# A fused two-convolution, joint-network forward and backward kernel: row-layout fe by a transposing transfer in every second chunk, x loaded without its halo block, a longer warm-up, and two weights on another queue

## The chip, the cores and the metric

The kernel runs on one core of one Trainium2 chip. The metric is the device time of one execution in microseconds. Times below are device times, or spans of the profiled execution where they are called that.

## What is computed

The reference computes a small speech network and the gradients of all its inputs with respect to a given `grad_out`. Cut to what matters:

```python
# x (2,16000,256)  w1,w2 (3,256,256)  g (2,8,256)  w_f,w_g,w_o (256,256), all bf16
h  = gelu(sum_i xp[:, i:i+T] @ w1[i])[:, ::2]     # 3-tap convolution, every 2nd row kept
f  = gelu(sum_i hp[:, i:i+T1] @ w2[i])[:, ::2]    # the same again: 4000 rows per batch
fe = f @ w_f;  ge = g @ w_g
j  = tanh(fe[:, :, None, :] + ge[:, None, :, :])  # (2,4000,8,256)
out = j @ w_o
# out_0 = out, then the gradients of x, w1, w2, g, w_f, w_g, w_o
```

The two batches of 4000 rows at quarter rate make 8000 rows in all. Every one of them has 8 values of `u` (the 8 rows of `g`), so the joint part (tanh, the product with `w_o` and its gradients) is eight times as large as the rows suggest.

## The kernel before

**Chunks.** The 8000 quarter-rate rows are cut into 17 chunks: 15 of 4 blocks of 128 rows (512 rows), one of 2 blocks of 128, and a last one of 64. Chunk 7 holds the border of the two batches. Tiles come in two layouts. In the column layout the 256 channels lie on the partitions (two halves of 128) and rows lie along the free axis; matmuls of the forward pass and of the input gradients read it. In the row layout 128 rows lie on the partitions; the weight gradients read it, since they contract over rows.

**Stages.** `stage_a(g)` does chunk g's forward part: `conv1` for the odd rows and then for the even rows of h, `conv2`, and the product with `w_f`, which gives FE in column layout (L607). `stage_j(g)` does the joint part in four pairs of two u's: JT = tanh(FE + GE) in column layout on ScalarE (L676), JR, the same values in row layout, by an addition of FER and GEB on VectorE (L700) and a tanh on ScalarE (L705), the products with `w_o` transposed (GOT) and with `w_o` (OUT), and the gradient of `w_o` (GWO, from JR and GO). `stage_de(g)` does the backward part: GN, GH, the gradients of the weights and of x. The loop at L1282 calls `stage_j(k)`, `stage_a(k+1)` and `stage_de(k-1)` together, so that three chunks are in work at any time.

**Who sets the order.** Nothing is issued as it is written. `op` records an operation with its engine or engines, a cost, a due time (`F.now` or `at`), what it reads and writes and which buffers it opens. `Flow.issue` (L108) then plays a list schedule: of all operations that could start it takes the earliest, with the due time as a tie-breaker (and as the choice among SyncE's transfers that could start within `NEAR` ns of the first), and emits each on its engine's in-order queue. Numbers such as `0.424 * dt`, `q * 0.813`, `NEAR`, `CROWD` and `KAPPA` belong to this planner and are in ns or in shares of a chunk; they move instructions but add none. Nearly all DMAs are issued by SyncE (SP), whose queue is in order too: an instruction that waits holds all that stand behind it.

**What the change touches.**

- `load_xc` (L405) brings x of a chunk in column layout into XC with one transposing transfer of 17 blocks of rows. Block 0 holds the row before each group of 16, which is the same data as block 16 shifted by one. `rows_xc` (L379) does chunk 0 in another way: four plain transfers into XL, TensorE transposes (L399), copies out of PSUM, and a GpSimd copy for block 0.
- `fe_rows` (L610) makes FER, the row layout of FE, by 8 TensorE transposes per chunk of four blocks (L622, 4 for the chunk of two) into one PSUM tile and one copy to SBUF by ScalarE or VectorE (`evac`, L624). Chunks 1 to 15 have it; chunk 0 makes JR from JT by transposes (L694), and the last chunk has its own code (`stage_j_last`).
- `tile_rows` (L535) makes a row layout by a transposing transfer from SBUF to SBUF on SyncE. HR, GNR and GHR are made so.
- `halo` (L477) copies a shifted block and a saved last column with GpSimd instructions of the form 128x254 and 128x2 (all on L357).
- At the start, `warm_up` (L1210) issues 14 matmuls on zeros, whose result nobody reads, and `unread` (L370, with `FILL = (1, 3)`) puts one more such matmul behind the transposes of the first XL tile and three behind those of the second. W1, WF and WG are loaded from ScalarE's queue, W2 and WO from SyncE's.

All matmuls stand on the helper's line L322, DMAs on L346 (transposing) and L348 (plain), copies out of PSUM on L331 and L333 (ScalarE) and L336 and L338 (VectorE).

Of the kernel before, what the change touches and what calls it, by code (L numbers as in the profile page):

```python
# [36 lines left out]
class Flow:  # L37
# [6 lines left out]
    NEAR = 9.118  # L44
    COLD = 6000.0
    CROWD = 9000.0
    KAPPA = 0.0287
# [170 lines left out]
def kernel(  # L218
# [28 lines left out]
    KT = 2  # L247
# [30 lines left out]
    for name, n in (("xc", 1), ("ht", 1), ("g1e", 2), ("g1o", 2), ("g2", 2), ("fe", 2),  # L278
                    ("fer", 2), ("gsq", 3), ("gs", 2), ("jt", 3), ("got", 3), ("go", 4), ("out", 3), ("jr", 3),
                    ("hr", 2), ("jsq", 2), ("ngz", 2), ("gh", 1), ("gn", 1), ("gnr", 1), ("ghr", 1), ("xr", 1), ("gx", 2),  # L280
                    ("hho", 2), ("hg1", 2), ("hgf", 2), ("hge", 2)):
# [89 lines left out]
    FILL = (1, 3)  # L371
# [10 lines left out]
    def rows_xc(c, XC, at):  # L382
# [3 lines left out]
        for h in range(nr // 4):  # L386
            XL, r0 = XLS[h // 2], 4 * (h % 2)
            src = xf[0:nr * P, :].rearrange("(p r) d -> p r d", r=nr)[:, 4 * h:4 * h + 4, :]
            xl_ops.append(dma("SP", lambda XL=XL, r0=r0: XL[:, r0:r0 + 4, :], lambda src=src: src, r=[], w=[(XL, h % 2)], bytes_=P * 2048,
                new=[XL] if h % 2 == 0 else [], load=True, at=at - 2.0, land=-400.0))  # L390
# [17 lines left out]
    def load_xc(g_, at, apart=0.0):  # L408
        c = chunks[g_]
        XC = st[g_]["XC"] = buf("xr" if c.first else "xc", [P, 17, KT, P], BF16, "XC")  # L410
        if c.first:
            return rows_xc(c, XC, at)
        cuts = ((0, 4 * c.nb + 1),)
        for n_, (b0, b1) in enumerate(cuts):
# [3 lines left out]
                land=1500.0 if g_ == 1 else 4500.0)  # L418
        if c.mid:
            pool_zero(lambda: XC[:, 0, :, c.pb:c.pb + 1], [], [(XC, ("m", 0))], at=at)  # L420
# [56 lines left out]
    def conv_gelu(g_, jobs, rd, h_buf, pre, ho, gname, gcls, gshape, gsave, news):  # L477
# [36 lines left out]
        late = F.now + CW * ({0: 1.024, 2: 0.207, 1: 1.404}.get(g_, 0.36))  # L514
# [34 lines left out]
    def stage_a(g_, t0, dt):  # L549
# [23 lines left out]
        F.now = t0 + 0.0781 * dt  # L573
# [3 lines left out]
        F.now = t0 + 0.00759 * dt  # L577
# [32 lines left out]
        F.now = t0 + 0.84 * dt  # L610
        tile_rows(g_, "HR", "hr", HT, 3 * nb + 1, shape=[P, 3 * NB + 1, D], land=4500.0)

    def fe_rows(g_):
        c, S = chunks[g_], st[g_]
        nb, n_, FE = c.nb, c.np, S["FE"]
        FER = S["FER"] = buf("fer", [P, NB, D], BF16, "FER")
        ps = psum(BF16)

        def trs(e, ps=ps):
            for a in range(nb):  # L620
                for kt in range(KT):
                    nc.tensor.transpose(out=ps[:n_, (a * KT + kt) * P:(a * KT + kt + 1) * P],  # L622
                                        in_=FE[:, kt, a * n_:(a + 1) * n_], identity=ident[:])
# [36 lines left out]
    def stage_j(g_, t0, dt):  # L660
# [4 lines left out]
        def cut(ap, lo, hi):  # L665
            return ap.rearrange("p (a n) -> p a n", a=nb)[:, :, lo:hi] if c.mid else ap

        def pair(up):
# [4 lines left out]
            for j in range(2):  # L673
                for mt in range(KT):
                    for k_, (lo, hi, b) in enumerate(parts_of(c)):
                        op("ACT", c_act((hi - lo) * nb, ptr=True), lambda e, j=j, mt=mt, lo=lo, hi=hi, b=b: nc.scalar.activation(  # L676
                            out=cut(JT[:, j, mt, :W], lo, hi), in_=cut(S["FE"][:, mt, :W], lo, hi), func=ACT.Tanh,
                            bias=GE[:, b, mt, 2 * up + j:2 * up + j + 1], scale=1.0),
                           r=[(S["FE"], mt), (GE, b)], w=[(JT, (j, mt, k_))],
                           new=[JT] if j == 0 and mt == 0 and k_ == 0 else [], at=tu - q * (0.813 - (2 * j + mt) / 4))  # L680
            npart = len(parts_of(c))
            for h in range(max(nb // 2, 1)):
                na = min(nb, 2)
                JR = buf("jr", [P, 2, 2, D], BF16, "JR")
                th = tu + q * (h / 2 - 0.656)
# [30 lines left out]
                gwo_ops.append(op("PE", c_pe([V] * (4 * na)), gwo, r=[JR, GO], w=[], at=tu + q * (h / 2 + 0.468) + DEFER.get((g_, up), 0.0)))  # L716
            OUT = buf("out", [P, NB, 2, V], BF16, "OUT_SB")
            for step in range(4):
# [12 lines left out]
                if d2 == 0:  # L731
                    JSQ = buf("jsq", [P, KT, CW], BF16, "JSQ")

                    def jsq(e, j=j, JSQ=JSQ):
# [5 lines left out]
                       r=[(JT, (j, mt, k_)) for mt in range(KT) for k_ in range(npart)], w=[JSQ], new=[JSQ], at=F.now - q * 0.269)  # L740
# [58 lines left out]
    def stage_j_last(t0):  # L799
# [7 lines left out]
        for u in range(U):  # L807
            for mt in range(KT):
                op("ACT", c_act(n_, ptr=True), lambda e, u=u, mt=mt: nc.scalar.activation(
                    out=JT[:, 0, mt, u * n_:(u + 1) * n_], in_=S["FE"][:, mt, :n_], func=ACT.Tanh,  # L810
# [124 lines left out]
    def stage_de(g_, t0, dt):  # L935
# [15 lines left out]
        F.now = t0 + dt * 0.07  # L951
# [68 lines left out]
        load_xr(g_, t0 - 300.0 if c.last else t0 + dt * 0.382, [got_op[0, UP - 1]] if c.first else ())  # L1020
# [170 lines left out]
    X1 = -258.2  # L1191
    W0 = chunks[0].W
    H0 = 263.4
    CONVS = 4
    LEAD = 0.403
    LATE = (100.0, 100.0, 100.0)
    DEFER = {(LAST - 1, 3): 100.0, (LAST - 1, 2): 130.0}
    EARLY = 0.0
    GEBX = 0.93
# [8 lines left out]
    WARM = 14  # L1208
# [14 lines left out]
    wload("ACT", WF, 0, lambda: WF[:], lambda: w_f.rearrange("(kt p) n -> p kt n", p=P), BIG, 4000.0)  # L1223
    wact([wload("ACT", WG, 0, lambda: WG[:], lambda: w_g.rearrange("(kt p) n -> p kt n", p=P), BIG, 4000.0)])
    for b in range(B):
# [3 lines left out]
        r=[], w=[(W2, i) for i in range(KK)], bytes_=393216, load=True, at=BIG - 1.0, land=1000.0, behind=[xl_ops[-1]])  # L1229
    dma("SP", lambda: WO[:], lambda: w_o.rearrange("(kt p) n -> p kt n", p=P), r=[], w=[(WO, 0)], bytes_=131072, load=True,  # L1230
# [115 lines left out]
```

## Time and profile before

| what | value |
|---|---|
| median of 3 runs | 768.4 us (768.23 to 768.64) |
| the profiled execution's own time | 769.64 us |
| its span, first to last instruction | 767.9 us |
| granted TensorE clock over the span | 1.00 |
| TensorE matmuls (PE) busy | 761.4 us, 99% |
| VectorE (DVE) busy | 714.5 us, 93% |
| ScalarE (ACT) busy | 700.2 us, 91% |
| GpSimd (POOL) busy | 76.7 us, 10% |
| HBM read, written | 53.52 MB, 50.35 MB |

The profiled execution is 1.24 us longer than the median of the unprofiled runs. PE is matmul work, PEld the weight loads that overlap it; "idle before" is the time an engine stood still ahead of an instruction, with what ended it. The share of the DMA engines in this profile can go over 1, since packets of one engine overlap. SPq, ACTq and POOLq are the issuing sequencers of those engines.

### The profile page before, as it was taken

How to read it: one execution, taken by the hardware profiler on the slowest of the kernel's cores; microseconds unless marked ns; L12 is line 12 of the kernel's file. 1: busy time of each engine (PE TensorE's matmuls, PEld its weight loads, DVE VectorE, ACT ScalarE, POOL GpSimd, SP SyncE). 2: the span in 40 equal slices, each digit the busy share in tenths (PEclk: the TensorE clock that was granted, in tenths of full speed). 3: DMA queues.
4: the chain of work that ended last, by engine and by line, in shares of the span. 5: the costliest groups of instructions: out<-in, count | busy, mean ns of one | idle time of the engine just before them, and what ended most of it. 6: DMA issues, size and time to landing. Idle time of an engine off the chain costs nothing.

```text
span 767.9 us, 15189 instructions
## 1 busy us (share of the span) xinstructions
PE 761.4 (99%) x5564; PEld 529.0 (69%) x5564; DVE 714.5 (93%) x1480; ACT 700.2 (91%) x1137; POOL 76.7 (10%) x222
## 2 busy tenths in 40 slices
PE   9999999999999999999999999999999999999998
PEld 6576676767767576675766767567576776777785
DVE  4999999899998999989999999998899989899996
ACT  5999999999898998999999999998989989998843
POOL 1101100020110100002000020110101101010100
PEclk9999999999999999999999999999999999999999
DMA  9999999999999999999999999999999999997966
GB/s 240 219 245 238 260 221 234 232 250 267 261 245 250 263 255 224 258 251 238 239 253 249 265 245 223 280 240 245 224 247 245 234 277 211 246 267 200 215 165 156
DMA packets 392431, 183.80 MB, mean 239 GB/s; under 512 B 315961, under 2 KB 385252, under 8 KB 390437
## 3 DMA queue, kind: packets, MB, share of 16 engines
q1 hardware_dynamic: 390210, 181.83, 103.7%
q10 hardware_dynamic: 2050, 0.98, 0.4%
q8 instruction: 43, 0.70, 0.4%
q14 instruction: 32, 0.26, 0.1%
q0 software_dynamic: 96, 0.02, 0.0%
HBM read 53.52 MB, written 50.35 MB: 135 GB/s over the span
## 4 chain that ended last, share of the span: by engine, by line
PE 95%; ACT 2%; DVE 2%; DMA 1%; issue 1%; POOL 0%; SPq 0%; DVEq 0%; ACTq 0%
PE ps L322 79%; PE GWO L322 14%; PE psb L622 1%; DMA XL<-in_x_dram 1%; PE psb L694 0%; ACT GX_SB L333 0%; DVE NGZ L745 0%; PE psb L399 0%; ACT JSQ L736 0%; ACT OUT_SB L331 0%; ACT JT L676 0%; DVE g_s L509 0%; PE psb L1242 0%; DVE GN L760 0%; DVE ZS L760 0%
## 5 line engine op out<-in xcount | busy, mean ns | idle before, releaser
L676 ACT ACTIVATE JT<-FE,GE 128x512 bf16<-128x512 bf16 (+3 forms) x272 | 184.5, 753 | 0.0
L322 PE MATMUL ps<-WO,JT 128*128 128x256 bf16 x1000 | 148.5, 273 | 0.0
L322 PE MATMUL ps<-GOT,WOT 128*128 128x512 bf16 (+1 forms) x516 | 147.4, 372 | 0.0
L745 DVE SCALAR_TENSOR_TENSOR NGZ<-JSQ,ps 128x512 f32<-128x512 bf16 (+2 forms) x238 | 146.6, 630 | 0.0
L705 ACT ACTIVATE JR<-JR 128x1024 bf16<-128x1024 bf16 x116 | 129.0, 1118 | 18.4 <-DVE JR L700 18.4
L322 PEld LDWEIGHTS <-JT 128*128 128x128 bf16 x1000 | 97.7, 98 | 59.0 <-issue 0.2
L331 ACT CAST OUT_SB<-ps 128x512 bf16<-128x512 f32 x204 | 128.3, 636 | 7.3 <-PE ps L322 5.9
L322 PE MATMUL GWO<-GO_R,JR 128*128 128x256 bf16 x1000 | 129.5, 273 | 0.7 <-ACT JR L705 0.7
L736 ACT ACTIVATE JSQ<-JT 128x1024 bf16<-128x1024 bf16 (+1 forms) x114 | 123.2, 1081 | 4.6 <-DVE NGZ L745 4.4
L760 DVE TENSOR_TENSOR ZS<-ZS,NGZ 128x1024 f32<-128x1024 f32 (+1 forms) x96 | 113.5, 1182 | 0.5
L322 PEld LDWEIGHTS <-JR 128*128 128x128 bf16 x1000 | 97.3, 98 | 20.5 <-ACT JR L705 2.1
L322 PEld LDWEIGHTS <-W 128*128 128x128 bf16 x624 | 59.2, 99 | 61.1 <-DVE GE L1266 0.5
L322 PE MATMUL ps<-W1T,GH 128*128 128x256 bf16 (+2 forms) x506 | 94.5, 325 | 0.0
L322 PE MATMUL ps<-XC,W 128*128 128x512 bf16 (+2 forms) x420 | 84.9, 359 | 0.0
L322 PE MATMUL ps<-GHR,XR 128*128 128x256 bf16 x744 | 84.3, 273 | 0.0
L700 DVE TENSOR_TENSOR JR<-FER,GEB 128x1024 bf16<-128x1024 bf16 x116 | 79.0, 683 | 2.8 <-PE GWO L322 2.8
L322 PEld LDWEIGHTS <-XR 128*128 128x128 bf16 x756 | 73.8, 98 | 9.3 <-issue 0.2
L916 DVE TENSOR_TENSOR ACC<-ACC,ps 128x512 f32<-128x512 f32 x87 | 57.6, 680 | 23.1 <-PE ps L322 23.0
L322 PEld LDWEIGHTS <-GH 128*128 128x128 bf16 (+1 forms) x506 | 49.5, 98 | 26.8
L333 ACT ACTIVATE GX_SB<-ps 128x512 bf16<-128x512 f32 (+1 forms) x95 | 62.5, 692 | 5.2 <-PE ps L322 5.0
L507 ACT ACTIVATE HT<-ps 128x512 bf16<-128x512 f32 (+2 forms) x102 | 62.9, 618 | 0.0
L505 ACT ACTIVATE g_sq<-ps 128x512 bf16<-128x512 f32 (+2 forms) x102 | 62.1, 610 | 0.7 <-PE ps L322 0.7
(138 smaller groups left out, 967.8 us busy)
## 6 DMA issues: line engine op xcount, KB each, us to landing
GO_R<-in_grad_out_dram SPq DMA_DIRECT2D x60, 512.0 KB, 5.2
out_dram<-OUT_SB SPq DMA_DIRECT2D x60, 512.0 KB, 4.5
out_dram<-GX_SB SPq DMA_DIRECT2D x30, 512.0 KB, 4.1
XR<-in_x_dram SPq DMA_DIRECT2D x14, 1088.0 KB, 8.5
GOT<-GO_R SPq DMA_TRANSPOSE x65, 5.3
XL<-in_x_dram SPq DMA_DIRECT2D x4, 256.0 KB, 3.7
GO_R<-in_grad_out_dram SPq DMA_DIRECT2D x4, 256.0 KB
out_dram<-OUT_SB SPq DMA_DIRECT2D x4, 256.0 KB, 2.7
```

What stands on the lines that cost most here:

```text
L322: nc.tensor.matmul(ps_ap, lhsT=lhsT, rhs=rhs, start=start, stop=stop)
L331: nc.scalar.copy(out=dst(), in_=src())
L333: nc.scalar.activation(out=dst(), in_=src(), func=ACT.Copy, scale=scale)
L505: op("ACT", c_act(W, True), lambda e, mt=mt, ps=ps: nc.scalar.activation(out=sq[:, 0:nb, mt, :n_], in_=blk(ps, c), func=ACT.Square, scale= ...
L507: op("ACT", c_act(W, True), lambda e, mt=mt, ps=ps: nc.scalar.activation(out=h_buf[:, ho:ho + nb, mt, :n_], in_=blk(ps, c), func=ACT.Gelu_ ...
L676: op("ACT", c_act((hi - lo) * nb, ptr=True), lambda e, j=j, mt=mt, lo=lo, hi=hi, b=b: nc.scalar.activation(out=cut(JT[:, j, mt, :W], lo, h ...
L700: op("DVE", c_dve(na * 2 * D, 0.5), lambda e, h=h, na=na, JR=JR: nc.vector.tensor_tensor(out=JR[:n_, 0:na], in0=S["FER"][:n_, 2 * h:2 * h ...
L705: op("ACT", c_act(na * 2 * D), lambda e, na=na, JR=JR: nc.scalar.activation(out=JR[:n_, 0:na], in_=JR[:n_, 0:na], func=ACT.Tanh), r=[JR], ...
L736: nc.scalar.activation(out=JSQ[:, :, :W], in_=JT[:, j, :, :W], func=ACT.Square)
L745: nc.vector.scalar_tensor_tensor(out=cut(Z[:, d2, :W], lo, hi), in0=cut(JSQ[:, d2, :W], lo, hi), scalar=1.0, in1=cut(ps[:, :W], lo, hi), o ...
L760: nc.vector.tensor_tensor(out=o_, in0=i0, in1=i1, op=ALU.add)
L916: op("DVE", c_dve(512), lambda e: nc.vector.tensor_tensor(out=acc_ap().rearrange("p k d -> p (k d)"), in0=acc_ap().rearrange("p k d -> p ( ...
```

## The change

Five things change.

1. **FER.** In chunks with an odd number (1, 3, ... 15) `fe_rows` makes FER with `tile_rows`, one transposing transfer of FE from SBUF to SBUF (8 blocks of 128x128, 4 in chunk 15). The transposes on TensorE and the copy out of PSUM are gone there. Even chunks (2, 4, ... 14) stay as they were. TensorE's transposes of FE fall from 116 to 56.
2. **FE's layout.** For that, FE is stored block by block (`[P, NB, KT, P]` in place of `[P, KT, CW]`). Its writers and its readers (the tanh of L676 and of the last chunk) now step over 4 pieces of 128 columns.
3. **XC without block 0.** In chunks 1 to 16 the transposing transfer of x starts at block 1 (16 blocks in place of 17; 4 in place of 5 in the last chunk). GpSimd copies block 0 from the last block and its first column from `hx`, a column saved from the chunk before: three more GpSimd instructions a chunk. The even convolution waits for them; the odd one doesn't read block 0.
4. **Warm-up.** 17 matmuls on zeros in place of 14, and 3 and 4 in place of 1 and 3 behind the transposes of the first two XL tiles. Six of the odd convolution's first matmuls now stand ahead of the third XL tile's transposes (all 12 of them stood behind), the other six behind the fourth's.
5. **WG and WF** are loaded from SyncE's queue, behind W2 and ahead of WO, and no longer from ScalarE's. WF's and WG's transposes move from ahead of the second half of the odd convolution to behind both convolutions.

The planner's numbers change with it, so that many instructions of all engines stand in another order: the product that makes FE is due at 0.279 of a chunk (0.424 before). The number of matmuls other than those named does not change.

```diff
-    NEAR = 9.118
+    NEAR = 116.4
-    CROWD = 9000.0
-    KAPPA = 0.0287
+    CROWD = 5300.0
+    KAPPA = 0.0264
...
-    FILL = (1, 3)
+    FILL = (3, 4)
...
         if c.first:
-            return rows_xc(c, XC, at)
-        cuts = ((0, 4 * c.nb + 1),)
+            rows_xc(c, XC, at)
+            return last_col(g_, XC, 2 * c.nb - 1, at)
+        cuts = ((1, 4 * c.nb + 1),)
...
+        last_col(g_, XC, len(cuts) - 1, at)
+        halo_xc(g_, XC, len(cuts) - 1, at)
+
+    def last_col(g_, XC, n_, at):
+
+        c = chunks[g_]
+        if not c.last:
+            hx = st[g_]["hx"] = buf("hx", [P, KT, 1], BF16, "hx")
+            pool_copy(lambda: hx[:], lambda: XC[:, 4 * c.nb, :, c.np - 1:c.np], 2, [(XC, ("m", n_))], [hx], new=[hx], at=at)
+
+    def halo_xc(g_, XC, n_, at):
+        c, ph = chunks[g_], st[g_ - 1]["hx"]
+        pool_copy(lambda: XC[:, 0, :, 1:c.np], lambda: XC[:, 4 * c.nb, :, 0:c.np - 1], 2 * c.np, [(XC, ("m", n_))], [(XC, "h")], at=at)
+        pool_copy(lambda: XC[:, 0, :, 0:1], lambda: ph[:], 2, [ph], [(XC, "h0")], at=at)
...
-        F.now = t0 + 0.424 * dt
-        FE = S["FE"] = buf("fe", [P, KT, CW], BF16, "FE")
+        F.now = t0 + 0.279 * dt
+        FE = S["FE"] = buf("fe", [P, NB, KT, P], BF16, "FE")
...
-            evac(lambda mt=mt: FE[:, mt, :c.W], lambda ps=ps: ps[:, :c.W], c.W, r=[ps], w=[(FE, mt)])
-        F.now = t0 + 0.617 * dt
+            evac(lambda mt=mt: FE[:, 0:nb, mt, :n_], lambda ps=ps: blk(ps, c), c.W, r=[ps], w=[(FE, mt)])
+        F.now = t0 + 0.542 * dt
...
     def fe_rows(g_):
         c, S = chunks[g_], st[g_]
         nb, n_, FE = c.nb, c.np, S["FE"]
+        if g_ % 2 == 1:
+            return tile_rows(g_, "FER", "fer", FE, nb, shape=[P, NB, D], at=F.now - FERQ, land=FERL)
...
-                            out=cut(JT[:, j, mt, :W], lo, hi), in_=cut(S["FE"][:, mt, :W], lo, hi), func=ACT.Tanh,
+                            out=cut(JT[:, j, mt, :W], lo, hi), in_=S["FE"][:, 0:nb, mt, lo:hi], func=ACT.Tanh,
...
-    WARM = 14
+    WARM = 17
...
-    wload("ACT", WF, 0, lambda: WF[:], lambda: w_f.rearrange("(kt p) n -> p kt n", p=P), BIG, 4000.0)
-    wact([wload("ACT", WG, 0, lambda: WG[:], lambda: w_g.rearrange("(kt p) n -> p kt n", p=P), BIG, 4000.0)])
+    wact(w1l[-1:])
...
+    for src_, dst_t in ((w_g, WG), (w_f, WF)):
+        dma("SP", lambda dst_t=dst_t: dst_t[:], lambda src_=src_: src_.rearrange("(kt p) n -> p kt n", p=P), r=[], w=[(dst_t, 0)],
+            bytes_=131072, load=True, at=BIG - 0.8, land=1000.0, behind=[xl_ops[-1]])
...
-            load_xc(k + 1, t0 - Wk * 0.21)
+            load_xc(k + 1, t0 - Wk * 0.234)
```

More of the change, by code (lines that the diff above doesn't have):

```diff
@@ L513, in conv_gelu @@
         N = KT * W
-        late = F.now + CW * ({0: 1.024, 2: 0.207, 1: 1.404}.get(g_, 0.36))
+        late = F.now + CW * ({0: 0.964, 2: 0.465, 1: 1.321}.get(g_, 0.431))
         go_ = 1 if gsave else 0
@@ L1198 @@
     EARLY = 0.0
+    FERQ = 273.5
+    FERL = 4236.0
     GEBX = 0.93
```

38 lines of the change are left out of this document (19 added, 19 removed).

## Prediction

> **What bounds the kernel now.** I read the page first (busy shares and the chain), then the engines by stretches, then what TensorE waited for. The page:
>
> ```profile
> span 767.9 us, 15189 instructions
> PE 761.4 (99%) x5564; PEld 529.0 (69%) x5564; DVE 714.5 (93%) x1480; ACT 700.2 (91%) x1137; POOL 76.7 (10%) x222
> PE 95%; ACT 2%; DVE 2%; DMA 1%; issue 1%; POOL 0%; SPq 0%; DVEq 0%; ACTq 0%
> ```
>
> TensorE is busy 99% and 95% of the chain that ends last. Two other engines are above 90%, so an average doesn't settle it; the stretches do (us from the start; busy time and count of PE, PEld, DVE, ACT, POOL; granted clock; DMA share; GB/s):
>
> ```profile
> 0.00:10.00 10.00, 8.42 (x51) 6.13 (x52) 1.44 (x4) 3.25 (x5) 2.04 (x10) 1.00 0.82 240
> 20.00:40.00 20.00, 19.88 (x152) 12.49 (x152) 20.00 (x44) 20.00 (x39) 2.31 (x7) 1.00 1.10 211
> 40.00:60.00 20.00, 20.00 (x175) 15.48 (x174) 20.00 (x41) 20.00 (x32) 0.00 (x0) 1.00 1.12 255
> 60.00:100.00 40.00, 39.08 (x266) 25.23 (x265) 39.53 (x81) 39.78 (x63) 5.29 (x15) 1.00 1.07 246
> 100.00:200.00 100.00, 100.00 (x713) 68.84 (x712) 96.10 (x189) 95.20 (x148) 8.58 (x24) 1.00 1.11 243
> 400.00:500.00 100.00, 100.00 (x698) 67.27 (x697) 95.32 (x187) 92.86 (x144) 10.71 (x28) 1.00 1.09 249
> ```
>
> From 100 us on TensorE has no gap at all, while DVE and ACT have 4 to 7% left. From 20 to 60 us DVE and ACT are full too. TensorE's waits, all of the run (total us, times, longest):
>
> ```profile
> PE ps L322 <- DVE g_sq L1203: 1.1, 1, 1.1
> PE GWO L322 <- ACT JR L705: 0.7, 2, 0.5
> PE psb L399 <- DMA XL<-in_x_dram: 0.5, 2, 0.3
> PE ps L322 <- POOL GN L357: 0.2, 1, 0.2
> ```
>
> The only transfer that ever held a matmul is XL, at the start. So there are two places where time can be had: matmuls taken out of the stream after 100 us, which count one for one, and the start.
>
> **1. Transposes of FE.** They fall from 116 to 56 (seven odd chunks with 8, one with 4). What one costs in the stream is read from the chain, where the group of 8 takes 0.45 us, that is 56 ns each; the group's mean of 219 ns holds the pipeline's latency, which the next matmul overlaps.
>
> ```profile
> 47.49 0.45 PE psb L622 x8
> L622 PE MATMUL psb<-ident,FE 128*128 128x128 bf16 x116 | 8.9, 219 | 0.0
> L331 ACT COPY FER<-psb 128x1024 bf16<-128x1024 bf16 x13 | 14.4, 1108 | 0.5 <-PE psb L622 0.5
> ```
>
> 60 x 0.056 = **-3.4 us** on the path. (The group's 8.9 us over 116 would give 77 ns and 4.6 us; it counts latency with no work behind it, so I take the chain's.) The copies of FER go as well: seven of 1.1 us and a half one, about 8.3 us, nearly all of ACT. ACT isn't the bound after 100 us, so this pays nothing there; it is the reserve for part 3.
>
> **2. The start.** Rows of the timeline up to the first activation (start, length):
>
> ```profile
> 0.74 4.38 SPq L348 DMA_DIRECT2D XL<-in_x_dram  x4
> 1.06 3.17 PE L322 MATMUL ps<-g_sq 128*128 128x256 bf16 x14 [1.06 <-DVE g_sq L1203]
> 4.46 1.03 PE L399 MATMUL psb<-ident,XL 128*128 128x128 bf16 x8 [0.23 <-DMA XL<-in_x_dram]
> 5.99 1.03 PE L399 MATMUL psb<-ident,XL 128*128 128x128 bf16 x8 [0.28 <-DMA XL<-in_x_dram]
> 8.31 2.27 PE L322 MATMUL ps<-XC,W 128*128 128x256 bf16 x12
> 10.42 0.61 PE L399 MATMUL psb<-ident,XL 128*128 128x128 bf16 x8
> 11.06 0.59 ACT L331 COPY XC<-psb 128x512 bf16<-128x512 bf16 x1 [1.92 <-PE psb L399]
> 12.34 0.60 ACT L505 ACTIVATE g_sq<-ps 128x512 bf16<-128x512 f32 x1 [0.68 <-PE ps L322]
> ```
>
> Eight transposes take 1.03 us at 4.46 and at 5.99, but 0.61 at 10.42: the matrix engine runs at half pace until about 10 us, though the stretch 0:10 shows a granted clock of 1.00; here spacing tells more than that column. TensorE was idle 0.23 and 0.28 us ahead of the first two XL tiles. The change fills those gaps (17 matmuls from 1.06 at 213 ns end at 4.7, past the first tile's arrival), so the pace should rise near 5 or 6 us. The Trainium skill, "TensorE: Matmul & The Clock Gate", Part 1 (The HAM clock gate), puts the change of pace after a full busy window of about 3.4 us, and lets the windows run free of the kernel's start. By that rule, as an estimate, the pace would rise between 4.5 and 7.9 us, varying by run; the trace agrees in that five microseconds with two gaps did not raise it.
>
> What then limits the first activation is XL's arrival. The fourth XL issue ends at 0.74 + 4.38 = 5.1, begins about 1.1 earlier, and a transfer lands 3.7 after its issue:
>
> ```profile
> XL<-in_x_dram SPq DMA_DIRECT2D x4, 256.0 KB, 3.7
> ```
>
> So the fourth tile is there between 7.7 and 8.8 us (with w_f and w_g out of its way, no later). From 8.8: 0.45 for its transposes, 0.8 for the slower copy out (0.59 and its latency), 0.65 for six matmuls of 256 (109 ns, from 0.87 us per 8 GWO matmuls in the chain below): 10.7 in place of 12.34, a gain of 1.6. From 7.7 it would be 2.7. If the pace rises no earlier than now, the waits still go but the matmuls don't shrink: about 0.5, or a small loss of as much where WG, WF and WO, now one behind the other on SyncE, come late. WG is first needed by the GE products near 16 us:
>
> ```profile
> 43.56 0.87 PE GWO L322 x8
> 16.56 0.35 PE L322 MATMUL ps<-gT,WG 128*128 128x8 bf16 x8
> 8.38 7.29 SPq L346 DMA_TRANSPOSE XC<-in_x_dram  x1
> 22.14 5.34 PE L322 MATMUL ps<-XC,W 128*128 128x512 bf16 x24
> ```
>
> WG and WF are 256 KB ahead of WO, the two GO_R and chunk 1's XC, under 1 us. XC's issue ends at 15.7 and is used at 22.14, so this is covered. I take **-1.5 us**, range +0.5 to -2.7; the stages behind it are full on three engines, so a shift at 12 us is carried on. The six added matmuls on zeros lie in time when TensorE waits for XL; if XL came earlier than that they would cost up to 6 x 0.21 = 1.3 us.
>
> **3. What is added, costed at nothing, and its cover.**
>
> ```profile
> 14.00:17.00 3.00, 3.00 (x38) 1.89 (x35) 2.67 (x8) 3.00 (x6) 1.29 (x4) 1.00 1.28 290
> GHR<-GH SPq DMA_TRANSPOSE x16, 5.2
> SPq L346 <- PE ps L322: 142.0, 42, 9.6
> L357 POOL COPY XC<-XC x1: 395/395/395, 11.7 to 11.7; 128x254 bf16<-128x254 bf16 x1
> L523 DVE TENSOR_SCALAR g_sq<-g_sq x51: 181/418/618, 17.9 to 741.0; 128x1024 bf16<-128x1024 bf16 x45, 128x512 bf16<-128x512 bf16 x3, 128x128 bf16<-128x128 bf16 x3
> L676 ACT ACTIVATE JT<-FE,GE 128x512 bf16<-128x512 bf16 x224 | 161.2, 791 | 0.0
> L676 ACT ACTIVATE JT<-FE,GE 128x416 bf16<-128x416 bf16 x16 | 11.4, 712 | 0.0
> ```
>
> *Transfers.* FER adds 60 blocks of 32 KB, block 0 takes 31 away: about 1 MB more. At 290 GB/s (14:17, transposing alone) that is 3.3 us of DMA over the run, and 0.9 us in an odd chunk. The DMA share is above 1 all along, so the engines have little idle time, yet SyncE's transposing issues wait 142 us for TensorE's matmuls to free buffers: the queue is ahead of its users. FER itself, half of a GHR, lands within 5.2 us of issue and FE is now made earlier in the chunk. Cost 0, upper end as the second rival.
>
> *GpSimd.* 48 more instructions (16 of 0.40 us, 32 short ones). They run beside DVE, 10% busy; but DVE's 418 ns operation is stretched to 618 in places, so a copy can hold DVE by 0.2 us. The Trainium skill, "SBUF — State Buffer", Who interferes with whom, says that GpSimd and certain DVE instructions take a shared port pair as an exclusive lock, which speaks against this change; the 618 agrees with it. At 0.2 us for each of 48 it is at most 9.6 us of DVE, against 4 to 7% idle (27 to 47 us over 670). Cost 0, upper end 1 us.
>
> *FE in blocks.* JT over 4 pieces of 104 columns took 712 ns where a straight line through the 791 for 512 at 0.83 ns a column gives 711. Nothing to 5 ns x 224, under the 8.3 us that ACT gains.
>
> **Sum.** 769.64 - 3.4 - 1.5 = 764.7 for an execution like the profiled one. That one is 1.24 above the median of the runs, so the median is forecast at **763.5 us**.
>
> **Rivals.**
>
> *Only the transposes pay* (the head gain is eaten by the first chunks, where DVE and ACT are full from 20 to 60 us and the chain runs through them): 768.4 - 3.4 = 765.0. For it: those 20.00 entries. Against: everything there starts from the activation at 12.34.
>
> *FER's transfer takes the transposes' place.* SyncE's queue is in order: FER waits there for FE, and GOT, XC and GO_R stand behind it. If TensorE then stands 0.43 us in each of 8 odd chunks, the 3.4 are gone and 766.9 is left; at 0.6, 768.3. For it: the DMA share near 1.1. Against: no matmul after the start ever waited for a transfer. That the change doesn't do what it says would look the same.
>
> *Slower: GpSimd's queue.* It is in order, and XC's halo copies wait for XC's transfer; GH's halo copy, which the matmuls of the x gradient need, stands behind them.
>
> ```profile
> 98.27 7.68 SPq L346 DMA_TRANSPOSE XC<-in_x_dram  x1
> 115.04 0.40 POOL L357 COPY GH<-GH 128x254 bf16<-128x254 bf16 x1
> 117.31 0.81 PE L322 MATMUL ps<-W1T,GH 128*128 128x512 bf16 x4
> ```
>
> GH's copy ends at 115.44 and is used at 117.31: 1.9 us of cover. It decides once XC lands over 1.9 us later than GH is ready; 0.6 us beyond it in each of 15 chunks is 9 us, giving 772.5. Against: XC's issue ended at 106, nine microseconds ahead.
>
> *More gain:* the 0.9 us that TensorE lost in 60:100 goes with ACT's relief, and the head gives 2.1: 762.0.
>
> **Chances.** Forecast 0.50, only the transposes 0.20, FER's wait 0.12, slower 0.09, more gain 0.09. About 0.2% (1.5 us) is what a measurement of this kernel can tell from no change. Faster takes the forecast, the first rival and the last: 0.79; within 0.2%: 0.12; slower 0.09. The range 761.5 to 767.5 holds the forecast with the head's bounds (762.3 to 765.5), both neighbours and half of the second rival.
>
> **What would show it.** L622's transposes x56; TensorE without gaps after 100 us; the first g_sq on ACT near 10.8 in place of 12.34, and eight XL transposes in 0.6 us from the second tile on; no wait of PE for FER, XC or POOL. It is wrong if PE's waits name DMA HR or JR behind FER, if GH's copies on POOL follow an XC wait, or if the time between fixed points in the middle (100 us to 700 us) doesn't shrink by 0.45 us per odd chunk.

## The result, and the profile after

| | before | after |
|---|---|---|
| median | 768.4 us (768.23 to 768.64, 6 runs) | 765.76 us (764.75 to 766.22, 6 runs) |
| ratio | | 0.9965, 95% interval 0.9955 to 0.9975 |
| the profiled execution | 769.64 us, span 767.9 | 765.80 us, span 763.9 |

The kernel became 2.64 us faster by the medians; the interval of the ratio allows 1.9 to 3.5 us. The forecast was 4.9 us, or 763.5 us. Set the two profiled executions side by side and the gain looks like 3.84 us. That comparison is wrong, and the reason is the main lesson of this case.

The page of after, the same three lines as before:

```profile
span 763.9 us, 15129 instructions
PE 756.5 (99%) x5510; PEld 525.3 (69%) x5510; DVE 716.0 (94%) x1479; ACT 699.2 (92%) x1130; POOL 94.4 (12%) x270
PE 89%; DVE 4%; ACT 3%; issue 2%; DMA 1%; POOL 0%; ACTq 0%; POOLq 0%; DVEq 0%
```

TensorE still bounds. Its 54 fewer instructions are 60 transposes less and 6 warm-up matmuls more. ScalarE stayed as busy as it was (699.2 against 700.2 us) although eight copies of FER left it (14 before, 6 now).

The stretches of after (us, then busy time and count of PE, PEld, DVE, ACT, POOL; granted clock; DMA share; GB/s):

```profile
0.00:10.00 10.00, 8.17 (x67) 6.33 (x68) 1.86 (x5) 3.40 (x6) 2.04 (x10) 1.00 0.83 235
20.00:40.00 20.00, 19.03 (x135) 11.78 (x134) 20.00 (x43) 20.00 (x37) 1.97 (x7) 1.00 1.11 208
40.00:60.00 20.00, 19.67 (x171) 15.04 (x169) 20.00 (x39) 20.00 (x33) 0.00 (x0) 1.00 1.11 255
60.00:100.00 40.00, 39.76 (x275) 26.50 (x276) 39.95 (x83) 40.00 (x64) 3.87 (x16) 1.00 1.07 254
100.00:700.00 600.00, 600.00 (x4252) 412.92 (x4250) 572.54 (x1153) 573.63 (x895) 75.39 (x198) 1.00 1.09 246
700.00:740.00 40.00, 39.51 (x348) 30.54 (x347) 37.99 (x106) 27.28 (x73) 5.13 (x19) 1.00 1.08 245
```

From 100 to 700 us TensorE has no gap, as forecast; the transposes of FE number 56. Three stretches have larger gaps than in the first profile of before: 20:40 (19.03, before 19.88), 40:60 (19.67, before 20.00) and 700:740 (39.51, before 40.00).

TensorE's waits in after (total us, times, longest):

```profile
PE ps L322 <- DVE g_sq L1222: 1.1, 1, 1.1
PE ps L322 <- DVE JR L336: 1.0, 1, 1.0
PE ps L322 <- DMA W<-in_w_dram: 0.8, 1, 0.8
PE GWO L322 <- ACT JR L722: 0.6, 1, 0.6
PE ps L322 <- POOL GN L357: 0.3, 1, 0.3
PE ps L322 <- DVE GN L976: 0.2, 1, 0.2
PE ps L322 <- DVE GNR L336: 0.2, 1, 0.2
```

The waits for XL are gone. In their place stands a wait of 0.8 us for W1, and a new one of 1.0 us for a copy of JR, which lies at 27.96 us. TensorE waits for neither FER nor XC, and its wait for GpSimd (0.3) is that for GN, which was there before (0.2). The head of after, TensorE and then ScalarE (start, length):

```profile
1.07 3.81 PE L322 MATMUL ps<-g_sq 128*128 128x256 bf16 x17 [1.07 <-DVE g_sq L1222]
4.67 1.06 PE L399 MATMUL psb<-ident,XL 128*128 128x128 bf16 x8
5.97 0.61 PE L399 MATMUL psb<-ident,XL 128*128 128x128 bf16 x8
8.39 0.39 PE L322 MATMUL ps<-XC,W 128*128 128x256 bf16 x2 [0.76 <-DMA W<-in_w_dram]
11.02 0.60 ACT L520 ACTIVATE g_sq<-ps 128x512 bf16<-128x512 f32 x1 [0.69 <-PE ps L322]
```

Eight XL transposes take 1.06 us at 4.67 and 0.61 us at 5.97: the pace rose between them, where the prediction had put it. The first activation starts at 11.02 in place of 12.34. So the head looks like a forecast that came true. The first experiment shows that most of its gain was never there to be had.

### The profile page after: what moved, and what is told of

The parts are those of the page before. It is cut to its first block, busy times and chain, and to the rows that moved or that the text cites. A ratio compares the mean times of both kernels' runs of the same rounds, so it can differ in the third digit from the quotient of the medians.

```text
span 763.9 us, 15129 instructions
## 1 busy us (share of the span) xinstructions
PE 756.5 (99%) x5510; PEld 525.3 (69%) x5510; DVE 716.0 (94%) x1479; ACT 699.2 (92%) x1130; POOL 94.4 (12%) x270
## 2 busy tenths in 40 slices
DMA packets 396400, 184.76 MB, mean 242 GB/s; under 512 B 319929, under 2 KB 389220, under 8 KB 394405
## 4 chain that ended last, share of the span: by engine, by line
PE 89%; DVE 4%; ACT 3%; issue 2%; DMA 1%; POOL 0%; ACTq 0%; POOLq 0%; DVEq 0%
PE ps L322 76%; PE GWO L322 13%; DMA W<-in_w_dram 1%; ACT OUT_SB L331 1%; DVE g_s L524 1%; ACT JSQ L753 1%; ACT JT L693 1%; ACT JR L722 1%; DVE NGZ L762 0%; PE psb L639 0%; DVE g_sq L536 0%; DVE JR L336 0%; DVE G L524 0%; DVE FE L336 0%; DVE ZS L777 0%
## 5 line engine op out<-in xcount | busy, mean ns | idle before, releaser
L722 ACT ACTIVATE JR<-JR 128x1024 bf16<-128x1024 bf16 x116 | 127.2, 1100 | 5.5 <-DVE JR L717 5.5
L753 ACT ACTIVATE JSQ<-JT 128x1024 bf16<-128x1024 bf16 (+1 forms) x119 | 128.0, 1076 | 3.7 <-DVE NGZ L762 3.6
L322 PE MATMUL ps<-W1T,GH 128*128 128x256 bf16 (+2 forms) x506 | 96.4, 325 | 0.0
L333 ACT ACTIVATE GX_SB<-ps 128x512 bf16<-128x512 f32 (+1 forms) x93 | 59.8, 667 | 11.9 <-PE ps L322 11.2
L520 ACT ACTIVATE g_sq<-ps 128x512 bf16<-128x512 f32 (+2 forms) x102 | 64.0, 629 | 1.0 <-PE ps L322 0.9
L522 ACT ACTIVATE HT<-ps 128x512 bf16<-128x512 f32 (+2 forms) x102 | 64.8, 638 | 0.0
```

The lines of the kernel that those rows point to most:

```text
L322: nc.tensor.matmul(ps_ap, lhsT=lhsT, rhs=rhs, start=start, stop=stop)
L333: nc.scalar.activation(out=dst(), in_=src(), func=ACT.Copy, scale=scale)
L520: op("ACT", c_act(W, True), lambda e, mt=mt, ps=ps: nc.scalar.activation(out=sq[:, 0:nb, mt, :n_], in_=blk(ps, c), func=ACT.Square, scale= ...
L522: op("ACT", c_act(W, True), lambda e, mt=mt, ps=ps: nc.scalar.activation(out=h_buf[:, ho:ho + nb, mt, :n_], in_=blk(ps, c), func=ACT.Gelu_ ...
L722: op("ACT", c_act(na * 2 * D), lambda e, na=na, JR=JR: nc.scalar.activation(out=JR[:n_, 0:na], in_=JR[:n_, 0:na], func=ACT.Tanh), r=[JR], ...
L753: nc.scalar.activation(out=JSQ[:, :, :W], in_=JT[:, j, :, :W], func=ACT.Square)
```

## The experiments

**1. Before once more.** No edit.

> The kernel before, unchanged, profiled once more. Theory: the profiled execution that the prediction was summed on (769.64 us) was a slow one of its kind, 1.24 us above the median, and the offset does not come with every profile: this one lies within 0.5 us of 768.4, and its trace shows less lost time than the first one between 55 and 85 us or in the half-paced matmuls of the first 10 us. Rival: a profile costs the kernel before 1.2 us each time, so it comes out at 769.4 to 769.9 again, with the same gaps.

Measured: 768.17 us (767.97 to 768.51, 10 runs), ratio 0.9999 (0.999 to 1.0008). Its profiled execution took 768.14 us, within 0.03 of the median. The timeline's first activation in it:

```profile
10.86 0.60 ACT L505 ACTIVATE g_sq<-ps 128x512 bf16<-128x512 f32 x1 [0.69 <-PE ps L322]
```

Then two fixed points in each of the two profiles of before, the transposes of JT in chunk 0 (26.1 and 27.6 us) and in the last chunk (first and last start, us). First the new profile:

```profile
L694 PE MATMUL psb<-ident,JT x64: 216/219/219, 26.1 to 48.4; 128*128 128x128 bf16 x64
L820 PE MATMUL psb<-ident,JT x8: 219/219/219, 740.0 to 740.4; 128*128 128x128 bf16 x8
```

And the profile that the prediction read:

```profile
L694 PE MATMUL psb<-ident,JT x64: 216/219/219, 27.6 to 49.9; 128*128 128x128 bf16 x64
L820 PE MATMUL psb<-ident,JT x8: 219/219/219, 741.5 to 741.9; 128*128 128x128 bf16 x8
```

The profile that the prediction read shows the same execution 1.5 us later, from 12 us to the end. Its head was 1.48 us late (12.34 less 10.86), and its own time lay 1.5 us above 768.14. Such a late execution is rare: of 33 runs of before taken beside experiments 1 to 4, two took 769.69 and 769.73 us and the others at most 768.59.

A late head is thus carried to the end one for one, as the prediction says. But the head that it took for before's is not the usual one. With the old start, the profiles of experiments 1, 6, 9 and 10 have their first activation at 10.86, 10.78, 11.20 and 10.93 us. With the new start, after and experiments 5, 8, 11 and 12 have it at 11.02, 10.48, 10.47, 10.38 and 10.62 us. By the middle values the new start is ahead by some 0.4 us (an estimate from these nine rows), which is no more than the differences inside either group.

**2 to 4. Parts alone, with the order planned anew.** The FER part put into before, the new start put into before, and after with the old start:

```diff
# b_fer: before, and in fe_rows
+        if g_ % 2 == 1:
+            return tile_rows(g_, "FER", "fer", FE, nb, shape=[P, NB, D], at=F.now - FERQ, land=FERL)
# b_new_start: before, with   (a_old_start: after, with the reverse)
-    FILL = (1, 3)
+    FILL = (3, 4)
-    WARM = 14
+    WARM = 17
...  # w_f and w_g from SyncE's queue, as in the change
```

> The kernel before with FE stored in blocks and FER of odd chunks by the transposing transfer, and nothing else of the change; its planner's numbers stay. Theory (the stream after 100 us is bound by TensorE, so each transpose taken out counts 56 ns): 765.0 us, 764.6 to 765.6, no gap of TensorE between 100 and 700 us. Rival (the transfer takes the transposes' place: TensorE waits about 0.3 us in each odd chunk): 766.5 to 768.4, with waits of PE for HR, GOT or JR behind FER.

> The kernel before with the start of the change alone: 17 matmuls on zeros, 3 and 4 behind the first two XL tiles, WG and WF on SyncE's queue. Theory (the first chunks are bound by VectorE from 20 to 60 us, and that chain eats the head's gain): the first g_sq comes about 1.3 us earlier, but the time falls by only 0 to 0.7 us: 767.7 to 768.4. Rival (the head's gain is carried to the end): 766.9 to 767.2.

> The changed kernel with the old start: 14 matmuls on zeros, 1 and 3 behind the XL tiles, WF and WG on ScalarE's queue. Theory (the gain of the start is eaten by the first chunks): 765.8 to 766.5, first g_sq near 12.3 us. Rival (the gain of the start is carried): 767.0 to 767.3.

Measured: b_fer 768.38 us (768.06 to 771.36, ratio 1.0007, 0.9999 to 1.0016); b_new_start 768.43 (767.8 to 769.21, ratio 1.0001, 0.9992 to 1.001); a_old_start 767.22 (766.34 to 770.4, ratio 0.9993, 0.9983 to 1.0003). The first missed the 3.4 us altogether. Its profiled execution took 770.07 us, 1.7 above its own median, so its waits needn't be those of an ordinary run. Three rows of TensorE's waits in it:

```profile
PE GWO L322 <- ACT JR L707: 1.8, 2, 1.0
PE ps L322 <- DVE ngb L1165: 1.3, 1, 1.3
PE psb L399 <- DMA XL<-in_x_dram: 1.2, 3, 0.6
```

The wait of 1.3 us lies at 754 us, in the last chunk. With 60 transposes fewer the list schedule puts everything else in another order too, and the kernel moves 2 MB more than before; which of the two took the gain is not parted here. In b_new_start the first activation came at 11.22 us. The median of a_old_start lies where a carried gain of the start would put it. But in its profiled execution (769.02 us, 1.8 above its median) TensorE waits for a transfer in the middle of the run (at 517, 565 and 613 us), which it does in the profiles of neither parent:

```profile
PE ps L322 <- DMA XR<-in_x_dram: 1.9, 3, 1.0
```

So these three don't tell what a part is worth, since each changes the plan together with the part. The following kernels therefore keep every other instruction in its place.

**5. After, with 60 matmuls put back.**

```diff
                 for kt in range(KT):
                     mm(ps[:, :c.W], WF[:, kt, mt * P:(mt + 1) * P], HT[:, oF:oF + nb, kt, :n_], kt == 0, kt == KT - 1)
+                if mt == 0 and g_ % 2 == 1 and g_ < LAST:
+                    for _ in range(2 * nb):
+                        mm(ps[:, :P], WF[:, 0, 0:P], HT[:, oF, 0, :], True, True)
```

> The changed kernel, every instruction in its place, with the transposes' load put back: 8 matmuls of 128 columns (4 in chunk 15), whose result is overwritten, ahead of FE's first product in each odd chunk, 60 in all. Theory (after 100 us TensorE is the bound, one for one): 60 x 0.056 = 3.4 us more, 765.8 to 769.1 us (768.8 to 769.4). Rival (another engine or the transfers hold the changed kernel, so TensorE has room): under 1 us more, up to 766.7.

Measured: 768.33 us (767.61 to 768.52), ratio 1.0 (0.9992 to 1.0009). With the matmuls back, all the rest of the change comes to nothing that can be told: the new start, XC without its block, the transfers, the new order, together 0.1 us from before (the interval allows 0.7 either way). The matmuls cost 2.57 us by the medians, where 60 x 0.056 would be 3.4. Two points that both kernels have, FE's transposes of chunk 2 and of chunk 14, show the price chunk by chunk. After first, then this kernel:

```profile
91.47 0.61 PE L639 MATMUL psb<-ident,FE 128*128 128x128 bf16 x8
651.53 0.61 PE L639 MATMUL psb<-ident,FE 128*128 128x128 bf16 x8
```

```profile
91.19 0.61 PE L642 MATMUL psb<-ident,FE 128*128 128x128 bf16 x8
653.98 0.61 PE L642 MATMUL psb<-ident,FE 128*128 128x128 bf16 x8
```

The way between them is 560.06 us in after and 562.79 here: 2.73 us for the six odd chunks 3 to 13, 0.45 us each, as forecast for the middle of the run.

**6. Before, with transposes taken out.**

```diff
-            for a in range(nb):
-                for kt in range(KT):
+            for a in range(nb if g_ % 2 == 0 else 1):
+                for kt in range(KT if g_ % 2 == 0 else 1):
...  # one transposed block is copied to all places of FER
```

> The kernel before, every instruction in its place, with 52 of the 60 transposes taken out: in odd chunks only the first of 8 (of 4 in chunk 15) is made and the copy reads it repeatedly, so FER holds wrong values there. Theory (one for one, and the order of the ends is unchanged, so nothing is given back): 52 x 0.056 = 2.9 us less, 768.3 to 765.4 us (765.1 to 765.8). Rival (the end of the kernel or the transfers take the gain back): 767.0 to 768.3.

Measured: 765.73 us (765.56 to 765.98), ratio 0.9967 (0.9956 to 0.9979): the whole gain, without any transfer. 52 were taken out. FER holds wrong values in the odd chunks; no other work is left out. Seven of the 52 are chunk 1's, at 46 us; its stretch 40:60 (the row below) has VectorE and ScalarE at 20.00 and TensorE at 19.19, so that a matmul less there is a gap more (19.54 in the second profile of before). The other 45 x 0.056 = 2.5 us is what was measured.

```profile
40.00:60.00 20.00, 19.19 (x163) 14.51 (x161) 20.00 (x40) 20.00 (x32) 0.00 (x0) 1.00 1.12 264
```

The transposes of chunks 2 and 14 say the same. The second profile of before, then this kernel:

```profile
95.28 0.61 PE L622 MATMUL psb<-ident,FE 128*128 128x128 bf16 x8
654.46 0.61 PE L622 MATMUL psb<-ident,FE 128*128 128x128 bf16 x8
```

```profile
95.20 0.61 PE L622 MATMUL psb<-ident,FE 128*128 128x128 bf16 x8
652.03 0.61 PE L622 MATMUL psb<-ident,FE 128*128 128x128 bf16 x8
```

At chunk 2 this kernel is 0.08 us ahead, and its first activation was already 0.08 us ahead (10.78 against 10.86): the seven transposes of chunk 1 brought nothing. From there to chunk 14 it gains 2.35 us, that is 42 x 0.056.

**7. After, with the old number of zeros.** 14 in place of 17, and 1 and 3 in place of 3 and 4, all else in its place.

> The changed kernel, every other instruction in its place, with 14 matmuls on zeros and 1 and 3 behind the XL tiles as before; WG and WF stay on SyncE's queue. Theory (the longer warm-up is worth nothing in a typical execution, since the first chunks are bound by VectorE): 765.4 to 766.2 us. Rival (the unbroken warm-up brings its 1.5 us): 766.9 to 767.4.

Measured: 765.67 us (764.89 to 766.81), ratio 0.9969 (0.9957 to 0.9981). The median is that of after: the zeros are worth nothing that can be measured. The profiled execution (766.81 us, the longest of its five) has its first activation at 10.09 us, the earliest of all. That lead of 0.93 us on after is still there at chunk 2's transposes (90.54 against 91.47) and has turned into a lag of 1.09 at chunk 14's (652.62 against 651.53). TensorE's gaps from 100 to 700 us make 0.8 of these 2.0 us, one of them a wait of 0.24 us for GOT; what the rest is stays open. So a lead at the start lasts only where nothing later stops the stream, and the middle of the changed kernel is not without a gap in every execution.

**8. After, with more transfers.** Behind FER's transfer a plain store of FE, 256 KB, to memory that nobody reads; some 2 MB over the run.

```diff
+                nc.sync.dma_start(out=SCR[g_ // 2][:, 0:nb].rearrange("p a k n -> p (a k n)"), in_=FE[:, 0:nb].rearrange("p a k n -> p (a k n)"))
```

> The changed kernel, every instruction in its place, and behind each FER transfer FE is also stored to scratch memory by a plain transfer, 256 KB in each odd chunk (128 KB in chunk 15), twice the transfer load that FER added. Theory (the transfers land ahead of their users): 765.8 us, at most 0.4 more. Rival (the transfers are as full as their share says, and each 256 KB costs its 0.9 us): 7.5 x 0.9 = 6.7 us more, 772.5; half of it still clearly shows.

Measured: 766.75 us (764.98 to 771.52), ratio 0.999 (0.9975 to 1.0005). Both expectations missed. The interval reaches from that of after to no change, so what the stores cost in the median is not settled. A transfer holds TensorE for 1.0 us, once, at 645 us (the helper's line is one further down in this kernel), and the times spread over 6.5 us where before spreads over 0.4 on the same chip.

```profile
PE ps L323 <- DMA GOT<-GO_R: 1.0, 1, 1.0
```

**9 and 10. Before's own order, with FER by transfer.** In the odd chunks 3 to 15, then in all of 3 to 15; the 52 or 100 transposes and their copies are replaced where they stand.

```diff
+            if g_ % 2 == 1 and g_ > 1:        # x7_kept_all: if g_ > 2:
+                nc.sync.dma_start_transpose(out=FER[:, 0:nb].rearrange("p a (k d) -> p (a k) d", d=P),
+                                            in_=FE[:, 0:nb].rearrange("p a k n -> p (a k n)"))
+                return
...  # FE in blocks, as in the change; the copies out of PSUM do nothing there
```

> The kernel before with its order kept on every engine, and only the FER part of the change: FE in blocks, and in chunks 3, 5, ... 15 the transposing transfer issued where the transposes stood; their 52 transposes and 7 copies are left out, chunk 1 keeps its own. Theory (one for one after the first chunks; the planner's new order, not the transfer, was what gave the gain back in the kernel with FER alone): 52 x 0.056 = 2.9 us less, 765.3 us (765.0 to 765.8). Rival (the transfer itself costs what the transposes cost): 767.0 to 768.4.

> The same with the transfer in every chunk from 3 to 15, even ones too: 100 transposes and 13 copies left out. Theory: 100 x 0.056 = 5.6 us less, 762.6 us, if the transfers (256 KB more in each chunk, none taken away) still land ahead of their users. Rival (the transfers have no more room): TensorE waits for GOT, XR or FER in the trace and the time is 765 us or more.

Measured: x6_kept_odd 767.65 us, in two groups, five runs at 765.36 to 765.93 and seven at 767.58 to 768.97 (ratio 0.9987, 0.9976 to 0.9998). The lower group has the gain of the transposes in full; only one of its runs was profiled, so what the upper group loses stays open. x7_kept_all took 770.87 us (770.05 to 774.1), ratio 1.0044 (1.0029 to 1.0059): 48 more transposes than in x6_kept_odd went, and it is slower than before. TensorE's longest waits there name VectorE:

```profile
PE ps L322 <- DVE NGZ L751: 2.7, 1, 2.7
PE ps L322 <- DVE GN L766: 2.3, 3, 1.1
```

VectorE, in turn, waited for FER's transfer, 8.6 us in three places. The longest of them is the one behind TensorE's 2.7 us:

```profile
DVE JR L706 <- DMA FER<-FE: 8.6, 3, 5.4
624.05 0.69 DVE L706 TENSOR_TENSOR JR<-FER,GEB 128x1024 bf16<-128x1024 bf16 x1 [5.41 <-DMA FER<-FE]
625.40 0.60 PE L322 MATMUL ps<-WO,JT 128*128 128x256 bf16 x4 [2.71 <-DVE NGZ L751]
```

FE was written by 599.6 us there, and FER's transfer was issued at 620.57, behind that of HR, which held SyncE's queue from 613.62 to 620.52. This is the second rival's mechanism, FER waiting in SyncE's queue, with VectorE between the transfer and TensorE.

**11 and 12. After, with block 0 back in x's transfer.** Experiment 11 does only that. Experiment 12 also sends GpSimd's copies elsewhere.

```diff
# x5_xc17 and x8_xc17_apart, in load_xc
-            dma("SP", lambda b0=b0, b1=b1: XC[:, b0:b1, ...
+            dma("SP", lambda b0=0, b1=b1: XC[:, b0:b1, ...
# x8_xc17_apart alone, in halo_xc
-        pool_copy(lambda: XC[:, 0, :, 1:c.np], lambda: XC[:, 4 * c.nb, :, 0:c.np - 1], ...
-        pool_copy(lambda: XC[:, 0, :, 0:1], lambda: ph[:], ...
+        pool_copy(lambda: NGR[:, :, 1:c.np], lambda: XC[:, 4 * c.nb, :, 0:c.np - 1], ...
+        pool_copy(lambda: NGR[:, :, 0:1], lambda: ph[:], ...
```

> The changed kernel, every instruction in its place, with block 0 back in the transfer of x (17 blocks in place of 16, 64 KB more per chunk, about 1 MB in all); GpSimd still copies it over. Theory (the changed kernel has a thin margin in its transfers, as with 256 KB more in every second chunk, which cost 1.0 us): 765.8 to 766.5. Rival (leaving block 0 out is what lets FER's transfer in, 1 MB against 2 MB): 767 us or more.

> The changed kernel, every instruction in its place, with block 0 again in x's transfer (17 blocks, about 1 MB more over the run), as in the run before it. Its GpSimd copies stay, but go to a tile that nobody reads by then, so that no copy has to wait for the transfer that brings block 0. This parts the two things that the run before mixed. If the 6.8 us there were GpSimd's queue (the copy of h's halo held in chunk 1, 4 us, and what followed from it), this kernel takes 765.8 to 767.0, its matmuls in chunk 1 don't wait 3.2 us for POOL, and the 1 MB costs no more than the 2 MB of the doubled transfer did (+1.0). If the 1 MB in front of the other transfers is what costs, it takes 769 to 772.5, and TensorE's waits name a transfer or what stands behind one (GOT, HR, XC).

Measured: x5_xc17 772.58 us (770.22 to 776.84), ratio 1.007 (1.0045 to 1.0094). The edit added a wait: the transfer now writes block 0, so GpSimd's copy of the first column has to stand behind it, and the copy of h's halo stands behind that in GpSimd's queue. GpSimd and TensorE in its timeline:

```profile
19.02 0.19 POOL L357 COPY XC<-hx 128x2 bf16<-128x2 bf16 x1 [8.74 <-DMA XC<-in_x_dram]
19.26 0.40 POOL L357 COPY HT<-HT 128x254 bf16<-128x254 bf16 x1
19.71 3.32 PE L322 MATMUL ps<-HT,W 128*128 128x512 bf16 x8 [3.23 <-POOL HT L357]
```

In after the same copies stand free of the transfer:

```profile
10.98 0.19 POOL L357 COPY XC<-hx 128x2 bf16<-128x2 bf16 x1
13.27 0.39 POOL L357 COPY HT<-HT 128x254 bf16<-128x254 bf16 x1
```

The transposes of chunk 2 come 4.09 us later there than in after (95.56 against 91.47), those of chunk 14 5.38 us later (656.91 against 651.53): most of the loss is this one stall.

Experiment 12 parts the wait from the megabyte: 767.6 us (765.95 to 772.18), ratio 0.9996 (0.9983 to 1.0008). (NGR holds a part of w_g's gradient from the middle of the run on: that kernel's w_g gradient lacks the first batch's share. No work is left out. The copies into NGR wait for nothing but x's transfer, 14.7 us once, as in after, 14.1.) The time is between its two expectations, nearer to the first. So of x5's 6.8 us about 5 are GpSimd's queue, and block 0's megabyte costs about 2 (1.84 by the two medians, 2.4 by the two ratios, 0.9996 and 0.9965, whose intervals don't meet). In its profiled execution (768.8 us, 1.2 above its median) TensorE waits for x itself at 20.5 us, VectorE waits 0.8 us for FER, and the middle of the run, closed in the profiles of before and after, has gaps:

```profile
PE ps L322 <- DMA XC<-in_x_dram: 0.9, 1, 0.9
PE ps L322 <- DVE GN L777: 0.6, 2, 0.3
```

```profile
400.00:500.00 100.00, 99.69 (x700) 67.84 (x699) 94.82 (x184) 96.22 (x149) 12.66 (x31) 1.00 1.07 245
600.00:700.00 100.00, 99.52 (x723) 69.95 (x721) 95.11 (x195) 93.94 (x151) 13.56 (x33) 1.00 1.07 245
```

That execution loses 2.1 us against after's between chunks 2 and 14 (it is 0.36 us behind at 91.83 and 2.48 at 654.01), but experiment 7's lost 2.0 us there with no more bytes than after. That the megabyte costs time therefore rests on the medians and intervals, not on these gaps.

The kernels in order of the megabytes that each moves (the DMA line of its page); x5_xc17, held by GpSimd, is left out:

| kernel | MB moved | transposes out | median (lowest to highest), us | runs |
|---|---|---|---|---|
| before (experiment 1) | 183.80 | 0 | 768.17 (767.97 to 768.51) | 10 |
| b_new_start, planned anew | 183.80 | 0 | 768.43 (767.8 to 769.21) | 11 |
| x2_take_out | 183.80 | 52 | 765.73 (765.56 to 765.98) | 5 |
| after | 184.76 | 60 | 765.76 (764.75 to 766.22) | 6 |
| x3_old_zeros | 184.76 | 60 | 765.67 (764.89 to 766.81) | 5 |
| x1_put_back | 184.76 | 60, 60 matmuls back | 768.33 (767.61 to 768.52) | 11 |
| a_old_start, planned anew | 184.76 | 60 | 767.22 (766.34 to 770.4) | 11 |
| x6_kept_odd | 185.51 | 52 | 767.65 (765.36 to 768.97) | 12 |
| b_fer, planned anew | 185.77 | 60 | 768.38 (768.06 to 771.36) | 11 |
| x8_xc17_apart | 185.78 | 60 | 767.6 (765.95 to 772.18) | 12 |
| x4_more_dma | 186.73 | 60 | 766.75 (764.98 to 771.52) | 12 |
| x7_kept_all | 187.06 | 100 | 770.87 (770.05 to 774.1) | 6 |

In after's own order, one megabyte over before shows no loss in the median, though the times of after and x3 spread by 1.5 and 1.9 us where those of x2 spread by 0.4. From some 185.5 on, the times spread by 3.3 to 6.5 us and their medians give back part of the gain or all of it. The sum of bytes isn't everything: a_old_start moves no more than after, stands in another order and spreads by 4.1 us, and 2 MB of plain stores (x4) have a lower median than 1 MB of transposing loads (x8), by less than their intervals can tell. That transposing transfers weigh more is a guess. The Trainium skill, "DMA: Bandwidth & Descriptors", Latency and other measured facts, gives a transposing transfer with steps in its middle dimension 261 GB/s. The trace doesn't bear this out as a bound: in 14:17 of before, with transposing transfers alone, 290 GB/s were moved. After's mean of 242 GB/s holds plain and transposing transfers, so how much room is left can't be read from it; the spread of the times and the waits for FER tell more.

## Why the prediction was right and wrong

The time is inside the range, and "faster" was right. The gain was forecast as 4.9 us and is 2.64. The time lies 2.3 us above the forecast and 0.8 above the first rival's 765.0, which had a chance of 0.20. The range held it because it was wide, and not because the start's term was right. Step by step:

- **1, transposes, -3.4: the mechanism right, the count too large.** 56 ns each holds, and so does 0.45 us per odd chunk in the middle (experiments 5 and 6). But chunk 1's eight run at about 46 us, where the prediction's own rows show VectorE and ScalarE at 20.00 of 20. In before's order they pay nothing (experiment 6). Put back in after's order they cost at most 0.3 us: from the first activation to chunk 2's transposes are 80.45 us in after (91.47 less 11.02) and 80.71 in experiment 5 (91.19 less 10.48). So the term was nearer to 52 x 0.056 = 2.9, and 2.5 and 2.6 were measured.
- **2, the start, -1.5: this step failed.** It read the head of one execution as what every execution pays. Before reaches its first activation at 10.86 in the other profile, and the new start is ahead by some 0.4 us in place of 1.5; taking the zeros out, with the order kept, moved the time by nothing that can be told. Worse, the delay was counted twice: the 1.24 us by which that execution lay above the median *were* the late head, and the sum took off the head's gain and then the 1.24 as well. By the median alone the sum would have been 768.4 - 3.4 = 765.0, the first rival's figure, though for another reason: the first chunks did not eat the head's delay (the late head was carried to the end), but there was little to gain. The wait for W1 (0.8 us in after, 0.3 in b_new_start) was not foreseen; in experiments 5, 8, 11 and 12, with the same start, it isn't there.
- **3, transfers at nothing: right, but on a thin cover.** No matmul waits for FER. What carries it is another part of the same change: the megabyte that block 0 no longer moves. With that put back (experiment 12) about 2 us are gone and the time is the second rival's. Its mechanism is to be seen in experiment 10, where VectorE waits 8.6 us for FER. The prediction summed the bytes, but costed the omission of block 0 only as one more edit at nothing.
- **GpSimd's copies at nothing: right.** POOL went from 76.7 to 94.4 us and TensorE doesn't wait for XC's copies. The "slower" rival did not happen. A copy that waits for x's transfer and holds the one behind it does exist: experiment 11 set it off, in h's halo copy in place of GH's. But it was one stall of 3.23 us in chunk 1 and not 0.6 us in each of 15 chunks; that both come to some 772.5 us is chance.
- **"From 100 us on TensorE has no gap at all": not at the end.** From 740 us on, TensorE is busy 24.15 of the 27.9 us left in the profile of before, and 20.35 of 23.9 in after. No term of the sum rests on it.
- **FE in blocks: right.** The tanh over 512 columns takes 773 ns against 780 in the second profile of before. ScalarE's expected relief of 8.3 us, however, is not there: the planner gave it 5 more squares of JT (119 in place of 114) and 8 more copies of OUT (212 in place of 204), 5 x 1.08 + 8 x 0.61 = 10.3 us.

```profile
L693 ACT ACTIVATE JT<-FE,GE 128x512 bf16<-128x512 bf16 x224 | 162.7, 773 | 0.1
```

The new order gives and takes. TensorE was without a gap in 700:740 before and loses 0.5 us there now, with a DMA share of 1.08 (0.86 before), and it loses 1.0 us at 28 us. Against that, the second profile of before has more gaps than after in 10:20, 40:60 and 60:100 (0.19, 0.46 and 0.48 us, where after has 0, 0.33 and 0.24). Experiment 5 puts the balance of all that isn't a transpose at 0.1 us, give or take 0.7.

The account of the error: 763.5 + 1.5 (start) + up to 0.5 (chunk 1's eight) = 765.5 at most. The 0.3 us or more that are left to 765.8 are not explained; by the interval of the ratio, a difference under 0.8 us can't be told here.

Open: what the upper group of x6_kept_odd waits for, why the middle of the changed kernel loses 2 us in one execution and nothing in another, and what WG's and WF's new queue or a single one of the planner's numbers is worth by itself.

## What to carry to other kernels

Before a late head in a profile is booked as a cost, set the profiled execution's own time against the median: where it lies above by about the size of the head's delay, the delay belongs to that run, and it may be taken off once or not at all. Count work taken out of the engine that bounds only where the others have slack, stretch by stretch, and check it between fixed points that both kernels have. Where work moves to transfers, look for the bytes that the same change takes away, and watch the spread of the times. Where a wait names an engine, look at what that engine waited for: in experiment 10 it was the transfer.

## What the runs showed of the hardware

The start's pace differs from run to run in the same kernel. In the second profile of before, the second and third XL tile's transposes:

```profile
5.73 0.85 PE L399 MATMUL psb<-ident,XL 128*128 128x128 bf16 x8
6.92 0.62 PE L399 MATMUL psb<-ident,XL 128*128 128x128 bf16 x8
```

The profile that the prediction read still had 1.03 us at 5.99, and its first activation came 1.48 us later. The granted clock's column showed 1.00 in both.

After TensorE stood still for 3.23 us in experiment 11, the granted clock fell (stretches of 2 us; the clock is the third number from the end):

```profile
20.00:22.00 2.00, 2.00 (x7) 0.63 (x6) 0.31 (x1) 1.43 (x3) 2.00 (x8) 0.50 1.14 212
22.00:24.00 2.00, 2.00 (x19) 1.44 (x18) 1.05 (x3) 1.07 (x3) 0.01 (x1) 0.65 1.07 192
```

The Trainium skill, "TensorE: Matmul & The Clock Gate", Part 1 (The HAM clock gate), has the clock at half rate after an idle window of about 3.4 us. This trace agrees in kind: 0.50 follows an idle time of 3.23 us, a little under that figure. A stall of that length therefore costs more than itself: here up to 1.7 us of slower matmuls came on top (an estimate: 2 us at 0.50 and 2 us at 0.65 lose 1.0 and 0.7).

GpSimd's copies did not all get slower with 48 more of them. Against the second profile of before, the 2-column copy out of GH took 878 ns in place of 641 on the mean and the one into HT 384 in place of 243, but the one out of G1o 603 in place of 653 and the one out of HT 214 in place of 279. VectorE's busy time rose by 1.4 us. TensorE's one wait for GpSimd went from 0.2 to 0.3 us.
